# Larger TensorE blocks for the first two batches' scores, the token fold and the row transposes of a fused attention and FFT-mixing kernel

## The chip, the cores and the metric

One core of one Trainium2 chip runs one launch of the kernel. The metric is the device time of that launch in microseconds (us), median of several runs. The kernel is a program written out in full: every engine (TensorE = PE, VectorE = DVE, ScalarE = ACT, GpSimd = POOL, SyncE = SP) has one long in-order list of instructions, with semaphores between them.

## The reference

Four batches, eight heads, 768 tokens, head size 64. Attention with a window of 96 tokens and 8 global tokens and a linear distance penalty; then, on the attention's output x (4 x 768 x 512), a two-dimensional FFT whose real part is added to x, a normalisation over the 512 features, and a two-layer network of 2048 hidden units.

```python
scores = scale * q @ k.T - slope[h] * dist          # kept: 0 <= i-j < 96, or j < 8
a = softmax(where(keep, scores, -1e9)); x = a @ v    # heads side by side: [B, 768, 512]
u = x + real(fft(fft(x, axis=1), axis=2))
un = (u - mean(u)) / sqrt(var(u) + 1e-6)
out = u + relu(un @ w_ch1) @ w_ch2
```

## The kernel before

**Stages.** For each batch b the work is: transposes of q and k (`trans`), scores and exponentials (`score`), weighted sums (`av`), a token fold of x (`fold_0` for batch 0, `fold_s` for the others) and a feature fold (`fold_d`), two DFT stages (`y_unit`, `u_unit`), transposes of the normalised rows (`nt_unit`), and the two layers (`ph_unit`, `pg_unit` or `pg_units`). The batches overlap: while the layers of one batch fill TensorE, the attention of the next is put between them. Heads are handled in pairs: hp = 0..3, and pair number n = 4 b + hp.

**What sets the order.** A table `ORDER` in the class `Plan` names, for every engine, its units or operations in sequence. PE's names are units: A is attention, M is the fold and DFT work, H the first layer, G the second. `A37` is the 38th attention unit; `M0.1` is the second operation that unit M0 asks of ACT or DVE. The tables are fixed. `Plan.run` only walks through them with prices for each operation; the prices decide in which of several PSUM buffers a unit's result goes, not the order on an engine. An engine waits at the head of its list until what that instruction needs is there.

**PSUM.** Before the layers start, four double banks ("xx" 0 and 1, "C", "D") serve all units in turn. A unit of PE can start when the bank it is given has been emptied by ACT or DVE.

**Scores of batches 0 and 1** (`score`, lines 704 to 782, with `pem` true). Each unit (b, hp, g) covers two of the six key blocks of 128 tokens (g = 0, 1, 2). The distance penalty is added by TensorE: four matmuls (line 729) in 64x64 blocks of the array multiply a scaled identity (`sid`) with a table of distances (`dist_sb`, both in the tile `misc`). Then the scores are added (line 743). The contraction is over 64 features, one head s of the pair in each half of the rows; the 128 keys of a block are cut into halves t, one in each half of the columns, so that four matmuls use four quarters of the array. For i > 0 the keys of the second 128 query columns come from `kB`, a copy of the keys with the global tokens put in (tile `mk`).

**Token fold of batch 0** (`fold_0`, lines 950 to 1039). Pairs 0 and 2 are folded by DVE (f1 to f4, with f5 on ACT). Pairs 1 and 3 (`PEF`) are folded by TensorE: for each of the two, unit `fold_pe(hp)` makes six sums of the six token blocks of x as 32 matmuls of 128 columns with a scaled identity as weights (line 1013), into one bank. M0 does pair 1, M1 pair 3. The result is copied out in two operations each (lines 1018 and 1020): M0.0, M0.1 and M1.0 on ACT, M1.1 on DVE. `norm` (lines 832 and 834) is the DVE operation that writes x of one pair, half of the token blocks at a time: A21.0 and A22.0 write pair 1, A23.0 and A24.0 pair 3.

**Order around the fold.** On PE: `... A23 A24 A37 A36 M0 A34 A25 M1 A35 M4 A28 A38 A26 M5 M2 ...`. A23 and A24 are the weighted sums of pair 3 of batch 0; A37 and A36 are scores of batch 1; A34 and A25 are transposes of batch 1; A35, A28 and A38 are scores of batch 1; M4 and M5 (`spread_unit`) place x for later; M2 is the first DFT unit. On DVE: `... A17.0 A22.0 A21.0 T.75 T.73 T.76 A23.0 A24.0 T.78 A34.1 T.79 T.74 T.80 M1.1 T.81 T.82 ...`, where T.80 and T.81 are the two halves of `g0`, the first step of the feature fold.

**Row transposes** (`nt_unit`, lines 1296 to 1324). For the three row groups of batch 0, 32 transposes of 64x64 blocks (line 1309) turn the normalised rows; the later groups are turned by DMA.

Of the kernel before, what the change touches and what calls it, by code (L numbers as in the profile page):

```python
# [24 lines left out]
class Plan:  # L25
# [9 lines left out]
    MIX = 1.3  # L35
    LANDED = {"HW": 0.55, "SW": 1.3}
    LAT = {"ACT": 0.14, "DVE": 0.12, "POOL": 0.08}
# [84 lines left out]
    def op_go(self, eng, name, start):  # L122
# [6 lines left out]
        if eng == "POOL":  # L129
            self.ports.append((start, end, 1 if dma else 0 if outs and outs[0][0] in ("vB", "kB") else 2))  # L130
        if dma:
            at = max(max(end + 0.55, 5.5) if eng == "POOL" else end + lat + 2.7 * (lat == 1.0 and end > 3.5), self.now)
# [19 lines left out]

    SHARED = {"kB": 1, "vB": 1, "sid": 1, "f1": 0, "f2": 0, "f3": 0, "z": 0, "g0": 0, "w": 0, "s": 0, "w2a": 0, "w2t": 0, "ex": 0}
# [3 lines left out]
    def beside(self, start, cost, kind):  # L157
# [4 lines left out]
        if names:  # L162
            s = self.op_start("POOL", names[-1])
            if s is not None:
                p = self.made[names[-1]]
                ports = ports + [(max(s, start), max(s, start) + p[0]["POOL"][0], 1 if p[7] else 0 if p[3] and p[3][0][0] in ("vB", "kB") else 2)]
# [15 lines left out]
    def move(self, go=False):  # L182
# [4 lines left out]
        both = [h[2] for k, h in act if k != "AQ" or sw]  # L187
        each = sum(both) * (self.MIX if len(both) > 1 else 1.0) / 1000.0
        rate = {k: h[2] / 1000.0 if k == "AQ" and not sw else each for k, h in act}
        t = min([self.now + h[1] * rate[k] for k, h in act] + [h[0] for k, h in heads if h[0] > self.now + 1e-9] + [self.NEVER])  # L190
        if not go:
            return t
# [3 lines left out]
        for k, q in self.q.items():  # L196
            if q and q[0][1] <= 1e-4:
                _, _, _, outs, uses, cell = q.pop(0)
                cell[0] = t + (1.3 + 0.4 * (t > 12) if k == "SW" else 1.1 if t < 8 else self.LANDED["HW"] + 0.7)
# [21 lines left out]
    def unit_start(self, unit):  # L221
# [7 lines left out]
        if not there:  # L229
# [114 lines left out]
def act(n):  # L344
    return 0.1 + n / 1180.0
# [10 lines left out]
def pool(n):  # L356
    return 0.16 + n / 1080.0


@with_exitstack  # L360
def kernel(
# [24 lines left out]
    PEF = (1, 3)  # L386
    CS = 2
# [130 lines left out]
    def load_v(b, hp):  # L518
        h0 = 2 * hp
        if b >= FB:  # L520
# [3 lines left out]
            swq(whole, 1.08, [("avdone", b - 2), ("wl", 7)], [("v", b, hp, t) for t in range(2)], (1536, 0.93), False)  # L524
            return
        if b == 1:
            for t in range(2 - hp % 2 * 2):
# [3 lines left out]
                swq(four, 1.08, [], [("v", b, hp, t), ("v", b, hp + 1, t)], (1536, 0.93))  # L531
            return
        for t in range(2):
# [3 lines left out]
            swq(run, 0.85, ([("avdone", b - 2), ("wl", 7)] if b > 1 else []), [("v", b, hp, t)], (768, 0.93), b < 2)  # L537
# [4 lines left out]
    def load_qk(b, hp):  # L542
# [3 lines left out]
        for w, src in enumerate((q, k)):  # L546
            if b >= FB:
                for h in range(2):
# [4 lines left out]
                    swq(run, 0.85, free(tag, ti) + [("wl", 7)], [("qk", n, w, h)], (768, 0.93), False)  # L553
# [25 lines left out]
            if n == 4:  # L579
# [5 lines left out]
                swq(two, 1.08, free(tag, ti), [("qk", n, w), ("qk", n + 1, w)], (1536, 1.53))  # L585
# [7 lines left out]
            swq(run, 0.85, free(tag, ti), [("qk", n, w)], (768, 1.53))  # L593
# [110 lines left out]
    def score(b, hp, g):  # L704
# [3 lines left out]
        def run(start, ring):  # L708
# [22 lines left out]
            for i, c0, cw in tiles:  # L731
                for s in range(2):
# [7 lines left out]
                    for q0, q1 in [(0, P), (P, 2 * P)][:cw // P] if i else [(0, 2 * P)]:  # L740
                        for t in range(2):
                            kt = kB[lo:lo + 64, n, i - 1, t, :] if q0 else TT[n][lo:lo + 64, 1, i * P + 64 * t:i * P + 64 * t + 64]
                            nc.tensor.matmul(pa[64 * t:64 * t + 64, s, c0 + q0:c0 + q1], kt,  # L743
                                             TT[n][lo:lo + 64, 0, i * P + q0:i * P + q1], start=not pem, stop=True,
                                             skip_group_check=pem, tile_position=(lo, 64 * t))
            e = pl.pe((0.45, 0.45, 0.34)[g] if pem else 0.24, start, "64x64" if pem else "64x32")
# [61 lines left out]
    def av(b, hp):  # L808
# [28 lines left out]
        def part(start, ring, x, k):  # L837
# [15 lines left out]
            pl.later([("DVE", 0.17 + 0.03 * m + m * dve(384), lambda: norm(po, k))], free(*XT[b]), e,  # L853
# [10 lines left out]
    def bounce(b):  # L864
# [26 lines left out]
        pl.later([("POOL", 1.1, rg)], xw + [("xr", b), ("c", "back")], 0.0, [("xg", b)], dma=(128, 4.94), rank=0)  # L891

    def fold_s(b):
# [3 lines left out]
        for n, (c0, cw) in enumerate(parts):  # L897
# [43 lines left out]
            pl.later([("DVE", (4 if b else 2) * dve2(cw), f3)], [("f2", b, n)], 0.0, [("f3", b, n)])  # L941
# [8 lines left out]
    def fold_0():  # L950
# [53 lines left out]
        def fold_pe(hp):  # L1004
            cols = slice(hp * P, (hp + 1) * P)

            def run(start, ring):
                zy()
                pf = bank(ring, f"pf_{hp}")
                for n, terms in enumerate(ZS):  # L1010
                    o = pf[:, n // 4, (n % 4) * P:(n % 4 + 1) * P]
                    for x, (w, i) in enumerate(terms):
                        nc.tensor.matmul(o, w, X[0][:, i, cols], start=(x == 0), stop=(x == len(terms) - 1))
                e = pl.pe(mm_us(P, 32), start)
                pl.used(("free",) + XT[0], e)
                zc = T[("z", 0)][:, :, cols]
                pv = pf.rearrange("p b (n m) -> p (b n) m", m=P)
                pl.later([("ACT", act(512), lambda: A(zc[:, 0:4], pv[:, 0:4], AF.Copy)), ("DVE", dve(512), lambda: V.tensor_copy(zc[:, 0:4], pv[:, 0:4]))],
                         [], e, [("z", 0, hp)], rank=0)
# [769 lines left out]
```

## Time and profile before

| what | value |
|---|---|
| time, median of 3 runs (lowest to highest) | 247.56 us (247.53 to 248.01) |
| the profiled execution: its time | 245.87 us |
| the profiled execution: span from first to last instruction | 244.1 us |
| mean granted TensorE clock in it | 0.991 |
| TensorE busy (matmuls) | 232.0 us, 3251 matmuls, and as many weight loads |
| DVE, ACT, POOL busy | 193.4, 138.8, 114.8 us |

The profile tells of one execution. "Busy" of PE is the time in which at least one matmul was under way from its first read to its modelled end, so that short pauses between groups do not show in it; the starts of the groups in the timeline do show them. A wait is put down to what released it; "issue" is time in which an engine waited for nothing that the profile knows of.

### The profile page before, as it was taken

The page shows a single profiled execution, that of the slowest core. Times are in us where ns is not written, and L with a number is a line of the kernel's source. Part 1 is how long each engine was busy: PE and PEld are TensorE (multiplying, and loading weights), DVE is VectorE, ACT ScalarE, POOL GpSimd, SP SyncE. Part 2 cuts the span into 40 slices and gives each one's busy share as a digit, 9 for nine tenths or more (in the row PEclk, how much of TensorE's full clock was granted, in tenths as well). Part 3 has the DMA queues.
Part 4 walks back from the last instruction along what each step waited for, and adds up shares of the span by engine and source line. Part 5 has one row for each costly group of instructions (what it writes and reads, how often), then busy time and mean ns, then how long its engine had stood idle before and what let it go on. Part 6 is the DMA issues. An engine that isn't in the chain of part 4 may idle for free.

```text
span 244.1 us, 7606 instructions
## 1 busy us (share of the span) xinstructions
PE 232.0 (95%) x3251; PEld 191.2 (78%) x3251; DVE 193.4 (79%) x420; ACT 138.8 (57%) x226; POOL 114.8 (47%) x164
## 2 busy tenths in 40 slices
PE   7679899999999999999999999999999999999993
PEld 2557776878677667788989888898889898888883
DVE  2559997879972789999999889889998755846483
ACT  2368788864657468658357788364534651434200
POOL 8998898866590038999059056500300320011020
PEclk9997999999999999999999999999999999999999
DMA  6999999999999999999999979220570330040212
GB/s 170 181 169 145 157 235 172 197 190 196 110 145 152 234 179 205 117 135 110 242 184 285 135 84 156 46 33 13 174 258 4 77 99 0 1 130 1 89 72 99
DMA packets 95938, 32.85 MB, mean 135 GB/s; under 512 B 84160, under 2 KB 92480, under 8 KB 95904
## 3 DMA queue, kind: packets, MB, share of 16 engines
q0 software_dynamic: 66176, 17.06, 71.7%
q1 hardware_dynamic: 26560, 12.56, 25.1%
q10 hardware_dynamic: 3168, 2.75, 4.1%
q8 instruction: 25, 0.41, 0.7%
q14 instruction: 9, 0.07, 0.1%
HBM read 31.44 MB, written 8.65 MB: 164 GB/s over the span
## 4 chain that ended last, share of the span: by engine, by line
PE 67%; DMA 14%; DVE 5%; ACT 5%; POOL 3%; issue 3%; SPq 1%; POOLq 0%
PE ph L1339 29%; PE pgD L1484 14%; PE pgA L1484 10%; DMA qk<-in_q_dram 4%; DMA v<-in_v_dram 4%; PE py L1105 3%; DMA hT<-in_q_dram 3%; PE pg L1370 3%; PE pav L822 3%; ACT ex L766 2%; DMA back<-backm 2%; DMA xr<-xd,back 2%; PE sc L737 2%; PE pu L1192 1%; ACT mk L1657 1%
## 5 line engine op out<-in xcount | busy, mean ns | idle before, releaser
L1339 PE MATMUL ph<-unT,w 128*128 128x256 f16 x768 | 94.4, 273 | 0.8 <-issue 0.4
L1339 PEld LDWEIGHTS <-w 128*128 128x128 f16 x768 | 73.6, 98 | 12.5 <-issue 1.2
L1344 ACT ACTIVATE hT<-ph 128x512 f16<-128x512 f32 x73 | 42.9, 596 | 54.6 <-PE ph L1339 52.6
L1484 PEld LDWEIGHTS <-hT 128*128 128x128 f16 x320 | 31.0, 98 | 4.3 <-issue 0.4
L1285 POOL TENSOR_SCALAR sm<-sm 128x2 f32<-128x2 f32 x12 | 3.4, 284 | 58.2 <-ACT un L1278 57.8
L763 ACT ACTIVATE er<-sc 128x1024 f16<-128x1024 f32 (+1 forms) x24 | 22.3, 951 | 11.4 <-PE sc L737 8.2
L1345 DVE TENSOR_SCALAR hT<-ph 128x512 f16<-128x512 f32 x23 | 15.7, 687 | 12.7 <-PE ph L1339 12.7
L766 ACT ACTIVATE ex<-sc 128x1024 f16<-128x1024 f32 (+1 forms) x24 | 21.7, 955 | 7.1 <-PE sc L743 6.9
L1502 DVE SCALAR_TENSOR_TENSOR u<-pgA,sm,u 128x256 f32<-128x256 f32 (+1 forms) x30 | 16.9, 568 | 6.4 <-PE pgA L1484 6.0
L1502 DVE SCALAR_TENSOR_TENSOR u<-pgD,sm,u 128x512 f32<-128x512 f32 (+1 forms) x21 | 15.2, 722 | 3.5 <-PE pgD L1484 3.3
L1355 POOL DMA_INDIRECT out_dram<-u,back x4 | 4.5, 1120 | 27.5 <-DVE rev L1140 16.3
L887 POOL DMA_INDIRECT xr<-xd,back x3 | 4.8, 1602 | 25.4 <-PE pg L1370 16.1
L1370 PE MATMUL pg<-w,hT 128*128 128x512 f16 x64 | 16.0, 379 | 0.0
L1118 ACT ACTIVATE zy<-py 128x1024 f16<-128x1024 f32 (+1 forms) x13 | 11.1, 857 | 8.4 <-PE py L1105 6.1
L778 DVE TENSOR_TENSOR ex<-er,mk 128x1024 f16<-128x1024 f16 (+1 forms) x24 | 15.1, 646 | 0.7 <-ACT er L763 0.7
L1278 ACT ACTIVATE un<-un 128x512 f16<-128x512 f16 x24 | 15.0, 625 | 1.1 <-DMA unT<-un 1.1
L552 POOL DMA_DIRECT2D qk<-in_k_dram x16 | 13.7, 903 | 1.2 <-DMA w<-in_moe_w_ch_dram 0.8
L1269 ACT ACTIVATE un<-u,sm 128x512 f16<-128x512 f32 x19 | 13.1, 717 | 1.9 <-DVE sm L1251 0.7
L552 POOL DMA_DIRECT2D qk<-in_q_dram x16 | 13.6, 870 | 0.0
L822 PEld LDWEIGHTS <-ex 128*128 128x128 f16 x352 | 12.4, 97 | 1.1 <-ACT ex L766 0.4
L834 DVE TENSOR_TENSOR x<-pav,rc 128x384 f16<-128x384 f32 x24 | 12.6, 554 | 0.6
L822 PE MATMUL pav<-v,ex 128*128 128x65 f16 x224 | 12.9, 193 | 0.2
(170 smaller groups left out, 492.9 us busy)
## 6 DMA issues: line engine op xcount, KB each, us to landing
w<-in_moe_w_ch_dram POOLq DMA_DIRECT2D x8, 512.0 KB, 13.4
out_dram<-u SPq DMA_DIRECT2D x15, 256.0 KB, 3.0
v<-in_v_dram POOLq DMA_DIRECT2D x12, 192.0 KB, 5.8
qk<-in_k_dram POOLq DMA_DIRECT2D x16, 96.0 KB, 5.4
qk<-in_q_dram POOLq DMA_DIRECT2D x16, 96.0 KB, 4.5
xr<-xd SPq DMA_DIRECT2D x3, 512.0 KB, 4.6
xd<-x ACTq DMA_DIRECT2D x2, 768.0 KB, 4.5
v<-in_v_dram POOLq DMA_DIRECT2D x8, 96.0 KB, 7.0
```

The costliest lines, as they stand in the source:

```text
L552: nc.gpsimd.dma_start(qk16[n][:, w, :, h], src[b, h0 + h].rearrange("(i m) d -> m i d", m=P))
L763: A(mine(), cut(pa), AF.Exp, 0.0, 0.125)
L766: A(cut(expst[hp][:, :, g * 512:g * 512 + (384 if g == 2 else 512)]), cut(pa), AF.Exp, 0.0, 0.125)
L778: VT(o, mine(), m, op=ALU.mult)
L822: nc.tensor.matmul(o[:, s * 65:(s + 1) * 65], lhsT, w, start=(a == 0), stop=(a == len(ops) - 1), skip_group_check=True)
L1278: A(x, x, AF.Square, accum_out=MV[c][:, a, 2:3])
L1339: nc.tensor.matmul(ph[:, a * CH:(a + 1) * CH].rearrange("p (x m) -> p x m", x=2), W1[0][:, d, jb * P:(jb + 1) * P], UNT[c][:, :, d, :], st ...
L1344: pl.later([("ACT", act(512), lambda: A(dst, ph, AF.Relu)), ("DVE", dve(512), lambda: V.tensor_scalar_max(dst, ph, 0.0))], [], e, [("h", c ...
L1345: ("DVE", dve(512), lambda: V.tensor_scalar_max(dst, ph, 0.0))],
L1370: nc.tensor.matmul(pg, HT[c][:, jb, t * P:(t + 1) * P], W2[0][:, jb, :], start=(jb == 0), stop=(jb == NJ - 1))
L1484: nc.tensor.matmul(o, lhs(j), rhs(j), start=(first and j == 0), stop=(j == NK - 1), skip_group_check=True)
L1502: V.scalar_tensor_tensor(o, x, r(t), acc, op0=ALU.mult, op1=ALU.add)
```

## The change

Three kinds of TensorE work are written in larger blocks.

1. *Scores of batches 0 and 1.* The score matmuls use blocks of 64 rows by 128 columns: one matmul covers all 128 keys of a block, where two covered 64 each. The penalty's four matmuls stay as they are, in 64x64 blocks. A unit has 12 matmuls instead of 20 (g = 1), or 10 instead of 16 (g = 0 and 2).
2. *Token fold of batch 0.* The two fold units no longer stand for a pair each. M0 makes the first four of the six sums for pairs 1 and 3 at once (24 matmuls of 256 columns), M1 the other two (8 of 256). M0 now needs x of both pairs. M0.0, M0.1 and M1.0, all on ACT, copy 512 columns each; DVE's M1.1 is gone.
3. *Row transposes.* Eight transposes of 128x128 in place of 32 of 64x64, into one bank, for three row groups.

That is 160 + 32 + 72 = 264 matmuls and 264 weight loads fewer. The tables of the order are otherwise the same. The prices of the planner are changed in many places (DMA rates and landings, ACT's fixed part, GpSimd's operations); they change no order, only which PSUM bank some units of batch 1 get. Two operations are offered to a further engine (`slow`, and `distk` on ACT), but no table names them there.

```diff
@@ score @@
-                    for q0, q1 in [(0, P), (P, 2 * P)][:cw // P] if i else [(0, 2 * P)]:
-                        for t in range(2):
-                            kt = kB[lo:lo + 64, n, i - 1, t, :] if q0 else TT[n][lo:lo + 64, 1, i * P + 64 * t:i * P + 64 * t + 64]
-                            nc.tensor.matmul(pa[64 * t:64 * t + 64, s, c0 + q0:c0 + q1], kt,
-                                             TT[n][lo:lo + 64, 0, i * P + q0:i * P + q1], start=not pem, stop=True,
-                                             skip_group_check=pem, tile_position=(lo, 64 * t))
-            e = pl.pe((0.45, 0.45, 0.34)[g] if pem else 0.24, start, "64x64" if pem else "64x32")
+                    own = TT[n][lo:lo + 64, 1, i * P:i * P + P]
+                    for q0, q1, kt in [(0, cw, own)] if i == 0 or cw == P else [(0, P, own), (P, cw, kB[lo:lo + 64, n, i - 1].rearrange("p t m -> p (t m)"))]:
+                        nc.tensor.matmul(pa[:, s, c0 + q0:c0 + q1], kt, TT[n][lo:lo + 64, 0, i * P + q0:i * P + q1],
+                                         start=not pem, stop=True, skip_group_check=pem, tile_position=(lo, 0))
+            e = pl.pe((0.65, 0.63, 0.44)[g] if pem else (0.33 if g == 0 else 0.21), start, "64x64" if pem else "64x32")
@@ fold_0 @@
-        def fold_pe(hp):
-            cols = slice(hp * P, (hp + 1) * P)
+        def fold_pe(part):
+            some = ZS[:4] if part == 0 else ZS[4:]
...
-                for n, terms in enumerate(ZS):
-                    o = pf[:, n // 4, (n % 4) * P:(n % 4 + 1) * P]
+                for n, terms in enumerate(some):
+                    o = pf[:, n // 2, (n % 2) * 256:(n % 2) * 256 + 256]
                     for x, (w, i) in enumerate(terms):
-                        nc.tensor.matmul(o, w, X[0][:, i, cols], start=(x == 0), stop=(x == len(terms) - 1))
+                        nc.tensor.matmul(o.rearrange("p (x m) -> p x m", x=2), w, X[0][:, i].rearrange("p (x y m) -> p x y m", y=2, m=P)[:, :, 1],
+                                         start=(x == 0), stop=(x == len(terms) - 1))
...
-            MIX.append(([("x", 0, hp, z) for z in range(2)] + [("sid", 1), ("hid",)], BANKS(0), run))
+            MIX.append(([("x", 0, hp, z) for hp in PEF for z in range(2)] + [("sid", 1), ("hid",)], BANKS(0), run))
@@ nt_unit @@
-                    for i in range(2):
-                        for h in range(2):
-                            r, o, x = slice(64 * i, 64 * i + 64), d * P + 64 * h, 64 * (a * ND + d)
-                            nc.tensor.transpose(pt[64 * h:64 * h + 64, i, x:x + 64], un[r, a, o:o + 64], idn[r, r],
-                                                tile_position=(64 * i, 64 * h))
+                    nc.tensor.transpose(pt[:, 0, (a * ND + d) * P:(a * ND + d + 1) * P], un[:, a, d * P:(d + 1) * P], idn)
@@ Plan.ORDER, DVE @@
-            "A24.0 T.78 A34.1 T.79 T.74 T.80 M1.1 T.81 T.82 A26.1 T.83 M2.1 M3.0 M9.1 M9.0 M7.0 M7.2 M7.1 M7.3 M8.0 M10.0 M8.2 M6.0 M11.0 M8.1 M8.3 M13.0 "
+            "A24.0 T.78 A34.1 T.79 T.74 T.80 T.81 T.82 A26.1 T.83 M2.1 M3.0 M9.1 M9.0 M7.0 M7.2 M7.1 M7.3 M8.0 M10.0 M8.2 M6.0 M11.0 M8.1 M8.3 M13.0 "
```

PE in one score unit (pair 0, g = 1), from the last of its four penalty matmuls on. Before:

```order
L729 MATMUL sc_1_207<-misc 64x512
L743 LDWEIGHTS qkT_170
L743 MATMUL sc_1_207<-qkT_170 64x128
L743 LDWEIGHTS qkT_170
L743 MATMUL sc_1_207<-qkT_170 64x128
L743 LDWEIGHTS mk
L743 MATMUL sc_1_207<-qkT_170,mk 64x128
L743 LDWEIGHTS mk
L743 MATMUL sc_1_207<-qkT_170,mk 64x128
```

And in the changed kernel (the first number of a shape is now 128, the keys of one matmul):

```order
L740 MATMUL sc_1_205<-misc 64x512
L753 LDWEIGHTS qkT_170
L753 MATMUL sc_1_205<-qkT_170 128x128
L753 LDWEIGHTS mk
L753 MATMUL sc_1_205<-qkT_170,mk 128x128
L753 LDWEIGHTS qkT_170
L753 MATMUL sc_1_205<-qkT_170 128x128
L753 LDWEIGHTS mk
L753 MATMUL sc_1_205<-qkT_170,mk 128x128
```

What was 64x64 throughout the unit now goes from 64x64 to 64x128 within it, and back at the next unit's penalty.

PE at the start of the first fold unit, M0, with the semaphores that an instruction waits for. Before:

```order
L743 MATMUL sc_1_690<-qkT_623,mk 64x128
L1013 LDWEIGHTS ident [waits DVE_49]
L1013 MATMUL pf_716<-x_383,ident 128x128 [waits PE_49]
L1013 LDWEIGHTS ident
L1013 MATMUL pf_716<-x_383,ident 128x128
```

And in the changed kernel:

```order
L753 MATMUL sc_1_610<-qkT_543,mk 128x128
L1023 LDWEIGHTS ident [waits DVE_49]
L1023 MATMUL pf_641<-x_343,ident 128x256 [waits PE_49]
L1023 LDWEIGHTS ident
L1023 MATMUL pf_641<-x_343,ident 128x256 [waits DVE_49]
```

The unit stands at the same place, and there is a second wait for DVE: the second matmul reads token block 3, which A24.0 writes for pair 3.

ACT around the fold. Before:

```order
L978 ACTIVATE zy_479<-ww_481 128x128 x2
L1018 ACTIVATE zy_479<-pf_716 128x4x128
L978 ACTIVATE zy_479<-ww_481 128x128 x2
L1020 ACTIVATE zy_479<-pf_716 128x2x128
L679 ACTIVATE qkT_861<-pt_800 128x1536
L1018 ACTIVATE zy_479<-pf_828 128x4x128
```

And in the changed kernel:

```order
L987 ACTIVATE zy_406<-ww_408 128x128 x2
L1034 ACTIVATE zy_406<-pf_641 128x4x128
L987 ACTIVATE zy_406<-ww_408 128x128 x2
L1034 ACTIVATE zy_406<-pf_641 128x4x128
L690 ACTIVATE qkT_733<-pt_696 128x1536
L1030 ACTIVATE zy_406<-pf_724 128x4x128
```

The sequence is the same; the fourth row copies 512 columns instead of 256, and the last is now the only copy of the second unit.

More of the change, by code (lines that the diff above doesn't have):

```diff
@@ L35 @@
     MIX = 1.3
+    ALONE = 1.54
     LANDED = {"HW": 0.55, "SW": 1.3}
-    LAT = {"ACT": 0.14, "DVE": 0.12, "POOL": 0.08}
+    LAT = {"ACT": 0.18, "DVE": 0.12, "POOL": 0.08}
     def __init__(self):
@@ L129, in op_go @@
         if eng == "POOL":
[L130 removed]
+            self.ports.append((start, end, 1 if dma else 0 if outs and outs[0][0] in ("vB", "kB", "ts", "w1s", "s") else 2))
         if dma:
[L132 removed]
+            at = max(max(end + 0.95, 5.33) if eng == "POOL" else end + lat + 2.7 * (lat == 1.0 and end > 3.5), self.now)
             cell = [self.NEVER]
@@ L190, in move @@
         t = min([self.now + h[1] * rate[k] for k, h in act] + [h[0] for k, h in heads if h[0] > self.now + 1e-9] + [self.NEVER])
+        if sw and nxt > self.now + 1e-9:
+            t = min(t, nxt)
         if not go:
```

108 lines of the change are left out of this document (60 added, 48 removed).

## The prediction

> **What bounds the kernel now.** I read the page's first part, then the windows of four stages, then PE's waits and its timeline up to 60 us.
>
> ```profile
> span 244.1 us, 7606 instructions
> PE 232.0 (95%) x3251; PEld 191.2 (78%) x3251; DVE 193.4 (79%) x420; ACT 138.8 (57%) x226; POOL 114.8 (47%) x164
> ...
> 36.00:56.00 20.00, 18.91 (x407) 14.92 (x402) 16.27 (x41) 15.49 (x23) 16.60 (x27) 1.00 1.87 186
> 56.00:76.00 20.00, 20.00 (x198) 14.76 (x197) 16.66 (x35) 11.34 (x23) 11.96 (x15) 1.00 1.76 147
> 106.00:240.00 134.00, 134.00 (x1603) 119.02 (x1599) 109.93 (x230) 67.53 (x119) 38.24 (x51) 1.00 0.60 104
> ```
>
> In a window's row the first number after the window is its length, the second PE's busy time; the last three are the granted clock, the DMA share and GB/s. From 56 us on PE is busy all the time, but for about 1 us between 76 and 106. So what arrives late at 56 us ends late by as much, and what counts is when PE gets there. All that is changed lies before, except two of the three groups of row transposes.
>
> Before 56 us PE has holes, and its waits name three without a releaser that matter, beside one for a DMA at the start:
>
> ```profile
> PE pt L652 <- DMA hT<-in_q_dram: 1.6, 1, 1.6
> PE pt L652 <- issue: 1.5, 1, 1.5
> PE py L1105 <- issue: 0.6, 1, 0.6
> PE ph L1339 <- issue: 0.4, 1, 0.4
> ```
>
> Counted in the timeline, the three stand after 223, 733 and 989 matmuls. The distances are 510 and 256, multiples of 128 but for two. Each matmul has a weight load, so 128 matmuls are 256 instructions: PE waits there for a block of its own program. The Trainium skill, "Runtime: NRT & Kernel Launch", section "Instruction fetch mechanics", says that an engine's program is refilled in blocks of 256 instructions and that the cost is mostly hidden. The trace agrees on the block and not on the hiding: the first hole is 1.53 us. Were it hidden, no hole could be saved, and the sum below would lose its two gains from holes and come to +3.05.
>
> ```profile
> 15.32 0.47 PE L652 MATMUL pt<-ident,hT 128*64 128x128 f16 x10
> 17.32 0.58 PE L652 MATMUL pt<-ident,hT 128*64 128x128 f16 x14 [1.53 <-issue]
> ...
> 14.42:17.83 3.41, 1.81 (x49) 1.37 (x45) 1.72 (x5) 2.01 (x3) 3.33 (x6) 1.00 2.27 163
> 17.83:21.24 3.41, 3.41 (x76) 2.40 (x76) 3.25 (x6) 2.44 (x3) 2.21 (x4) 0.50 1.98 164
> ...
> 17.95 0.96 DVE L676 COPY qkT<-pt 128x1536 f16<-128x1536 f16 x1 [1.74 <-PE pt L652]
> ```
>
> The hole cuts the transposes of pair 1 of batch 0 (A6) in two. DVE waits for them until 17.95 and has no pause after that until 30.2. And 3.41 us after the hole run at half clock.
>
> **The score blocks.** Four matmuls in 64x64 blocks, with 128 columns each, start every 0.055 us: the four quarters work at once.
>
> ```profile
> 43.10 0.36 PE L729 MATMUL sc<-misc 64*64 64x384 f16 x4
> ...
> 43.45 0.33 PE L729 MATMUL sc<-misc 64*64 64x384 f16 x4
> 43.61 0.23 PE L743 MATMUL sc<-qkT 64*64 64x128 f16 x4
> 43.67 0.23 PE L743 MATMUL sc<-qkT,mk 64*64 64x128 f16 x4
> 43.73 0.23 PE L743 MATMUL sc<-qkT 64*64 64x128 f16 x4
> 43.88 1.07 PE L1192 MATMUL pu<-t,zy 128*128 128x128 f16 x16
> ```
>
> In 64x128 blocks two work at once on twice the keys, which is the same rate if the two row halves overlap as they do now. So 160 pairs of instructions fewer save no array time. They add changes of block shape. Two units of the same kind stand here: the first, followed by another 64x64 unit, takes 43.45 - 43.10 = 0.35; the second, followed by 128x128 work, takes 0.43. A change of shape costs 0.08. It does so too where only the columns change:
>
> ```profile
> 29.47 0.86 PE L652 MATMUL pt<-ident,qk 128*64 128x128 f16 x24
> 30.16 0.84 PE L652 MATMUL pt<-ident,tt 128*64 128x128 f16 x24
> 30.93 0.56 PE L1013 MATMUL pf<-x,ident 128*128 128x128 f16 x7
> ```
>
> 24 transposes take 0.69 before more of the same shape, and 0.77 before 128x128. The Trainium skill, "TensorEngine Tiling (Array Packing)", section "Key Properties", says that a change of the tiling mode, not of the tile, drains TensorE; it gives no time. By it the change from the penalty's blocks to the scores' must cost something, and the trace's 0.08 agrees. I take 0.09, since two heads that run one after the other within a unit also leave a short tail at each drain. No row shows 64x64 to 64x128; bounds are 0 (a column switch at no cost) and 0.12 (the longest such step I find).
>
> Each of the 24 units gets one change more inside, and a second where the next unit also is in 64x64 blocks. After the fold there are ten units (A35 A28 A38 A39 A29 A32 A33 A40 A31 A27) and five such neighbours (A35-M4, A28-A38, A39-A29, A33-A40, A31-M6): 15 x 0.09 = **+1.35**.
>
> **The fold.** What matters is when it may start.
>
> ```profile
> 26.79 0.56 DVE L834 TENSOR_TENSOR x<-pav,rc 128x384 f16<-128x384 f32 x1
> 28.70 0.56 DVE L834 TENSOR_TENSOR x<-pav,rc 128x384 f16<-128x384 f32 x1
> 29.40 0.56 DVE L834 TENSOR_TENSOR x<-pav,rc 128x384 f16<-128x384 f32 x1
> 30.44 0.96 DVE L676 COPY qkT<-pt 128x1536 f16<-128x1536 f16 x1 [0.22 <-PE pt L652]
> ...
> 27.58:29.47 1.89, 1.89 (x32) 1.78 (x32) 1.00 1.40 195
> 55.20 1.75 PE ph L1339 x16
> ```
>
> The last rows are the first fold unit's stretch and the chain's piece of 16 layer matmuls of 256 columns. The columns to work through are the same: 64 matmuls of 128 in two units of 1.89, or 32 of 256. At 1.75/16 = 0.109 us, 24 take 2.62 and 8 take 0.87, with a change of shape each 3.67 for 3.78: **-0.1**.
>
> M0 starts at 27.58, right after pair 1 is written (26.79 + 0.56 = 27.35). Now it needs pair 3 too, whose last write ends at 29.96: 2.38 later. Behind the waiting M0 stand, on PE's list, A34, A25, M1 and all that follows; DVE needs A34's result for the copy at 30.44 and then idles, ACT needs A25's. Nothing can pass, so this goes straight to the end unless DVE gets there earlier.
>
> It does, by the first hole. In the changed kernel A6 ends after 197 matmuls, so that it lies wholly ahead of the 223rd, where the hole now is; by then two more score units are issued, and the block has had more time to come. A6 then needs 24 x 0.028 = 0.67 from its start. Its start moves back: six score units ahead of it have ten changes of shape, 0.9, of which I let 0.5 count, since some of these units wait for ACT or DVE anyway. It ends near 16.5 in place of 17.7, and DVE, without a pause from there on, can be 1.1 earlier at A24.0 if the last v of batch 0 is there when DVE comes to copy it.
>
> ```profile
> 16.23 0.75 POOL L535 DMA_DIRECT2D v<-in_v_dram  x1
> ...
> DMA to landing us min/median/max: 5.8/7.0/7.4
> ...
> 23.70 0.29 DVE L793 COPY vB<-v 128x528 f16<-128x528 f16 x1
> ```
>
> It is issued at 16.23, so it lands from 22.0 to 23.6; DVE would come at 22.6. I let the 1.1 stand: M0 starts near 28.9, **+1.3**. Bounds: +2.4 (no gain from the hole) and +0.7 (all of 1.7 us).
>
> The order of the rest fits: with M0 done at 31.6 and M1 at 34.1, ACT's copies run about 2 us later than now, DVE's g0 too, and the first DFT unit finds its banks and its operands at about 38.7, when PE comes to it (37.23 now).
>
> **What is given back.** Between the starts of A28 and A38 lie 1.18 us:
>
> ```profile
> 33.93 0.39 PE L729 MATMUL sc<-misc 64*64 64x512 f16 x4
> ...
> 35.11 0.41 PE L729 MATMUL sc<-misc 64*64 64x512 f16 x4 [0.32 <-DVE zy L1020]
> ```
>
> A28's matmuls need 0.44 (four of 512 columns at once, 0.215, and four times 0.055). A38 waits for the bank that M1.1 empties; M1.1 is gone, and M1.0 empties it on ACT at about 35.6, before PE comes there (36.4). Of the 0.74 I take back **-0.4**; the rest is a wait for a copy of keys, which may stay. Bounds 0 and -0.7.
>
> The holes of 0.56 and 0.38 us: fewer instructions per microsecond leave more time for each block, but the boundary at the 733rd matmul falls among layer matmuls only 6 us after the one before, and the hole at the 989th came 6.6 us after its predecessor. One of two stays: **-0.5**. Bounds 0 and -0.94.
>
> The row transposes:
>
> ```profile
> 47.02 0.47 PE L1309 MATMUL ptu<-ident,un 64*64 64x64 f16 x32
> 47.42 0.28 PE L1192 MATMUL pu<-t,zy 128*128 128x128 f16 x2
> 53.83 0.45 PE L1309 MATMUL ptu<-ident,un 64*64 64x64 f16 x32
> 54.36 0.33 PE L822 MATMUL pav<-v,ex 128*128 128x65 f16 x5
> ```
>
> A group takes 0.40 to 0.53 now. Eight of 128 columns at 0.056 (a fold unit's 1.89 less a change, over 32) take 0.45, and two groups lose the change of shape on entering: **-0.2** in all.
>
> Sum: +1.35 - 0.1 + 1.3 - 0.4 - 0.5 - 0.2 = +1.45. The profiled execution's own time is 245.87 (span 244.1 and 1.77 around it); it becomes 247.3. The median of the runs is 247.56, 1.69 above that execution; with it the forecast is **249.0 us**.
>
> **The rivals.**
>
> *The row halves don't overlap in 64x128 blocks.* For it: nothing in the trace runs in such blocks. Against it: row halves overlap in the 64x64 units. The scores of a unit would take twice their 0.22 (g = 0, 1) or 0.165 (g = 2): after the fold 7 x 0.22 + 3 x 0.165 = 2.0, and the units before A6 would undo the 1.1 gained there. 249.0 + 3.1 = 252.1. Chance 0.12.
>
> *The wait ahead of the fold slows the clock.* PE, done with A36 near 26.7, idles until 28.9. The window with the 1.53 us hole was followed by 3.41 us at 0.50; a second such stretch costs up to 1.7: 250.7. Against it: the 1.6 us for the DMA ended at 9.48 and were not followed by one:
>
> ```profile
> 8.00:16.00 8.00, 6.09 (x184) 4.69 (x184) 5.29 (x12) 5.52 (x7) 7.88 (x15) 1.00 2.05 170
> ```
>
> The Trainium skill, "TensorE: Matmul & The Clock Gate", Part 1, asks a whole idle window of about 3.4 us for this, by which there would be none; the row at 17.83 speaks against that rule, since its predecessor was half busy. Chance 0.18.
>
> *Faster: the switch from the penalty to the scores is free.* Only the column split changes there, and the rows keep theirs. If it costs under 0.03, the 1.35 goes and A6 ends another 0.5 earlier; with the second of the later holes gone too (0.44): 249.0 - 2.3 = 246.7. Against it: 29.47 to 30.93 above. It decides once the price is below 0.03. Chance 0.20.
>
> *Nothing to measure:* the waits around 28 to 36 us absorb the fold's wait, as DVE's chain turns out 1 us earlier still. 247.6. Chance 0.08.
>
> **How the numbers follow.** Forecast 249.0 with chance 0.42, its own range 248.1 to 250.0. Half a microsecond (0.2%) is about what this measurement can tell from none. Faster 0.20 (the free switch), same 0.09 (the last rival and a little of the forecast), slower 0.71 (forecast, clock, row halves). The range reaches down to the free switch, 246.5, and up past the slower clock, 251.4, leaving out the row halves and the outer parts.
>
> **What would show it.** The timeline should have the first fold matmuls after a PE wait of 1 us or more for DVE's L843, starting near 29; DVE's copy of A6 near 16.7; a hole of issue after the 223rd matmul under 0.5 us and no half clock before 21; 0.08 to 0.1 us between the last penalty matmul's columns and the first score; 0.055 us between starts of pairs of 64x128 matmuls. It is wrong if M0 starts before 28.3, if that step is under 0.03, or if A6 is cut by a hole again.

## The result, and the profile after

| kernel | median of the runs, us | runs | to before, with its 95% interval |
|---|---|---|---|
| before | 247.55 (244.93 to 250.14) | 14 | |
| changed | 250.16 (249.02 to 252.95) | 14 | 1.0144 (1.0104 to 1.0183) |

By the medians the change makes the kernel 2.6 us slower; by the ratio it is 1.44%, or 3.6 us. Here and below, medians count all runs, while the ratio leaves out runs more than 1.5% above the fastest of their kernel, so that a tail of late runs shows in the median alone. The first two rows of the changed kernel's page:

```profile
span 250.6 us, 7075 instructions
PE 237.1 (95%) x2987; PEld 190.6 (76%) x2987; DVE 193.6 (77%) x419; ACT 138.6 (55%) x226; POOL 114.2 (46%) x164
```

There are 531 instructions fewer, and PE is busy 5 us longer. The profiled execution is one of the longest of its 14 (252.34 us), so its 6.5 us over the profiled execution of before are not the median's 2.6. Part of the rest is found below.

PE's waits, with the engine and the line waited for, then us in all, times and the longest:

```profile
PE pf L1023 <- DVE x L843: 2.4, 2, 2.0
...
PE pav L831 <- ACT unT L1329: 1.1, 1, 1.1
PE sc L748 <- DVE u L1262: 0.8, 1, 0.8
```

Two things stand out. No row with "issue" is left among PE's waits, where before had 2.5 us in the three main ones. And the fold now waits for the division of pair 3; further on, two units wait that did not before. The timeline of PE, start and length in us, then what it does and in brackets the idle time ahead of it:

```profile
26.69 0.41 PE L740 MATMUL sc<-misc 64*64 64x512 f16 x4
27.04 0.23 PE L753 MATMUL sc<-qkT 64*128 64x128 f16 x2
27.10 0.22 PE L753 MATMUL sc<-qkT,mk 64*128 64x128 f16 x2
27.16 0.22 PE L753 MATMUL sc<-qkT 64*128 64x128 f16 x2
27.21 0.22 PE L753 MATMUL sc<-qkT,mk 64*128 64x128 f16 x2
29.43 0.28 PE L1023 MATMUL pf<-x,ident 128*128 128x256 f16 x1 [1.99 <-DVE x L843]
30.12 0.81 PE L1023 MATMUL pf<-x,ident 128*128 128x256 f16 x6 [0.41 <-DVE x L843]
...
32.84 0.42 PE L1023 MATMUL pf<-x,ident 128*128 128x256 f16 x1
33.05 0.42 PE L1023 MATMUL pf<-x,misc 128*128 128x256 f16 x1
33.26 0.42 PE L1023 MATMUL pf<-x,hid 128*128 128x256 f16 x1
```

The same stretch by windows (length, PE's busy time with its matmuls, and so on; the granted clock is the third number from the end):

```profile
27.44:29.43 1.99, 0.00 (x1) 0.01 (x1) 1.96 (x10) 1.54 (x4) 1.99 (x4) 1.00 1.49 177
29.43:31.05 1.62, 1.22 (x10) 0.94 (x11) 0.86 (x4) 0.00 (x0) 1.62 (x3) 1.00 0.95 132
31.05:34.46 3.41, 3.41 (x20) 2.16 (x20) 0.00 (x0) 0.10 (x1) 0.55 (x1) 0.50 1.11 267
34.46:36.77 2.31, 2.31 (x56) 1.94 (x52) 1.46 (x3) 2.18 (x5) 0.44 (x1) 1.00 2.51 198
```

PE stands still from 27.44 to 29.43. 1.6 us after it has begun again it runs at half clock for 3.41 us, just while the fold is in work: its matmuls start 0.21 us apart (32.84, 33.05, 33.26), where 0.109 was expected. With the wait of 0.41 for pair 3's second division, the first fold unit takes 4.8 us until the transposes behind it start (34.25). VectorE and ScalarE meanwhile run dry, as the row of VectorE's copy behind it shows; the others are what decides when the fold may start:

```profile
17.41 0.95 DVE L687 COPY qkT<-pt 128x1536 f16<-128x1536 f16 x1
20.06 0.30 DVE L802 COPY vB<-v 128x528 f16<-128x528 f16 x1 [0.76 <-DMA v<-in_v_dram]
...
28.81 0.56 DVE L843 TENSOR_TENSOR x<-pav,rc 128x384 f16<-128x384 f32 x1
...
29.51 0.56 DVE L843 TENSOR_TENSOR x<-pav,rc 128x384 f16<-128x384 f32 x1
...
35.31 0.96 DVE L687 COPY qkT<-pt 128x1536 f16<-128x1536 f16 x1 [4.98 <-PE pt L663]
```

The last division of pair 3 ends at 29.51 + 0.56 = 30.07. It ended at 29.96 before: in this execution VectorE has gained nothing.

PE's loss against before, taken at the starts of the same unit in the two profiled executions, is 1.2 us at 13.8 us: half of it, 0.61, is there at the transposes that wait for a DMA at the start (10.09 for 9.48), the rest comes from five changed score units. It is -0.5 at 23.7, since the first hole and before's half clock behind it are gone, +1.85 at the first fold unit, +4.8 at the transposes behind it (0.9 of this is only work that moved from the second fold unit into the first), +4.0 at the first DFT unit, +3.6 at the second row transposes, +4.8 at the pav that follows, +5.1 at 140.9 us, +6.1 at 141.4 and 6.5 at the end (times of the kernel before).

### The profile page after: what moved, and what is told of

It is laid out like the page before. It is cut to its first block, busy times and chain, and to the rows that moved or that the text cites. A ratio compares the mean times of both kernels' runs of the same rounds, so it can differ in the third digit from the quotient of the medians.

```text
span 250.6 us, 7075 instructions
## 1 busy us (share of the span) xinstructions
PE 237.1 (95%) x2987; PEld 190.6 (76%) x2987; DVE 193.6 (77%) x419; ACT 138.6 (55%) x226; POOL 114.2 (46%) x164
## 4 chain that ended last, share of the span: by engine, by line
PE 68%; DVE 14%; DMA 12%; POOL 2%; ACT 2%; issue 1%; DVEq 0%; SPq 0%
PE ph L1349 26%; PE pgD L1497 12%; PE pgA L1497 9%; PE pav L831 3%; DMA xd<-tt 3%; DMA v<-in_v_dram 3%; PE pg L1380 3%; PE py L1119 3%; DMA out_dram<-u 3%; PE pz L1659 2%; PE pu L1206 2%; DMA unT<-un 2%; DMA xr<-xd 2%; PE pf L1023 2%; DVE u L1515 2%; PE sc L748 1%
## 5 line engine op out<-in xcount | busy, mean ns | idle before, releaser
L1299 POOL TENSOR_SCALAR sm<-sm 128x2 f32<-128x2 f32 x12 | 4.8, 400 | 64.8 <-ACT un L1292 64.5
L787 DVE TENSOR_TENSOR ex<-er,mk 128x1024 f16<-128x1024 f16 (+1 forms) x24 | 15.7, 669 | 1.1 <-ACT er L772 1.1
L896 POOL DMA_INDIRECT xr<-xd,back x3 | 3.6, 1196 | 25.0 <-PE ph L1349 16.5
L687 DVE COPY qkT<-pt 128x1536 f16<-128x1536 f16 (+1 forms) x6 | 5.3, 887 | 10.0 <-PE pt L663 6.8
```

The costliest lines, as they stand in the source:

```text
L787: VT(o, mine(), m, op=ALU.mult)
```

## The experiments

Two theories stood at first: F, that the fold, as one unit for both pairs, carries the loss, and S, that the changes of shape in the score units do. Each kernel ran beside runs of before on the same chip. "Clock loss" is one minus a run's mean granted clock, times its time, averaged over the runs: a stretch of 3.41 us at 0.50 counts 1.7 us. It is 1.05 us for before (96 runs beside the experiments; two more, at 302 and 598 us, are left out) and 2.19 us for the changed kernel (14 runs).

| experiment | median, us | before beside it | ratio and interval | clock loss, us | runs |
|---|---|---|---|---|---|
| fold alone | 251.81 | 247.66 | 1.0160 (1.0115 to 1.0204) | 2.65 | 6 |
| scores alone | 247.55 | 247.66 | 0.9993 (0.9960 to 1.0026) | 1.22 | 12 |
| row transposes alone | 247.28 | 247.66 | 1.0011 (0.9977 to 1.0046) | 0.78 | 12 |
| changed, fold by pairs | 249.20 | 247.66 | 1.0046 (1.0002 to 1.0091) | 1.13 | 12 |
| changed, fold two units later | 250.87 | 248.15 | 1.0107 (1.0032 to 1.0182) | 1.67 | 6 |
| changed, wait filled | 248.99 | 248.15 | 1.0070 (1.0035 to 1.0104) | 0.44 | 12 |
| changed, norms swapped | 249.78 | 248.15 | 1.0116 (1.0056 to 1.0176) | 2.05 | 6 |
| prices alone | 247.81 | 248.15 | 1.0004 (0.9960 to 1.0048) | 0.62 | 12 |
| changed, pair 3 divided first | 250.04 | 248.05 | 1.0059 (1.0016 to 1.0102) | 1.23 | 12 |
| the same, and norms swapped | 248.89 | 248.05 | 1.0000 (0.9959 to 1.0042) | 0.52 | 13 |
| before, pair 3 divided first | 247.15 | 248.05 | 0.9957 (0.9925 to 0.9989) | 0.95 | 12 |
| scores and row transposes | 248.86 | 246.94 | 1.0034 (0.9987 to 1.0081) | 0.92 | 12 |

### Which of the three parts costs the time

Four kernels take the change apart. Three make one part of it in the kernel before, at before's prices:

```diff
fold alone:            + fold_pe(hp // 2), two units of 256 columns, and no M1.1 on VectorE
scores alone:          + nc.tensor.matmul(pa[:, s, c0 + q0:c0 + q1], kt, ..., tile_position=(lo, 0))
row transposes alone:  + nc.tensor.transpose(pt[:, 0, ...], un[:, a, d * P:(d + 1) * P], idn)
```

The fourth is the changed kernel with before's fold:

```diff
- fold_pe(hp // 2)
+ fold_pe(hp)
```

> The kernel before with the new token fold alone (24 + 8 matmuls of 256 columns, M0 after both pairs). Theory F (the loss is the wait ahead of the fold and the half clock that follows it): M0 waits 2 us or more for the last write of x of pair 3, a stretch of 3.4 us at half clock may follow, and the time is 2 to 4 us over that of before. Theory S (the loss is the changes of block shape in the score units): no more than 0.5 us over.

> The kernel before with the scores of batches 0 and 1 in 64x128 blocks alone. Theory S: a step of 0.13 us within each of 24 units and 0.10 between neighbours, about 4.5 us in all, of which 2 to 3 us reach the end. Theory F: the ten units after the fold add 1.8 us, the program's holes that go give 1 us or more back, and the time is within 1 us of before.

> The kernel before with the row transposes in 128x128 blocks alone. Both theories: 0 to 0.5 us faster, three groups of 0.45 us without a change of block shape on either side.

> The changed kernel with the fold put back to one unit for each pair (scores, transposes and prices as changed). Theory F: 2 to 4 us under the changed kernel, about the time of before. Theory S: within 1 us of the changed kernel, 249 to 251 us.

The fold alone loses 4.15 us by the medians, a little more than theory F had said and more than the whole change; by the ratios (1.0160 and 1.0144) the two can't be told apart. Scores alone, where theory S wanted 2 to 3 us, and row transposes alone move nothing that can be measured. The fourth kernel is less clear: its ratio falls from 1.0144 to 1.0046, which is 2.4 us and what theory F said, but its median is only 1.0 us below the changed kernel's, in the range of theory S. So the fold by itself carries the loss, as theory F has it, and the score blocks by themselves do not; what is left with before's fold is taken up under "Scores and row transposes together". The fold-alone kernel's waits show what it has besides the fold's wait:

```profile
PE pf L1014 <- DVE x L834: 2.1, 2, 1.7
...
PE pav L822 <- issue: 1.5, 1, 1.5
...
PE pt L652 <- issue: 0.9, 1, 0.9
PE ptu L1314 <- issue: 0.9, 1, 0.9
```

It has the wait ahead of the fold and keeps holes of issue as well, and its clock loss is the largest of all, 2.65 us. The trace of scores alone has no hole: with the pairs of instructions that the blocks save, the holes go. The other traces agree. In the five kernels with before's score blocks (before itself, fold alone, row transposes alone, prices alone, before with pair 3 divided first) every hole of 0.2 us or more stands after 223, 350, 733, 861 or 989 matmuls, whatever unit is there; the distances are multiples of 128 but for one or two. In the nine with the new blocks there is none. That scores alone is no faster all the same fits the changes of shape: 24 units at 0.13 us for the change inside (26.69 to 27.04 in the timeline above, less 0.215 for the matmuls) are 3.1 us, part of it beside other waits, against holes of 2.5.

### Is it the wait, and can the wait be filled with other work?

The two fold units go behind the two units of transposes that stood behind the first of them, and ScalarE's copies with them:

```diff
 PE:  A37 A36
- M0 A34 A25 M1
+ A34 A25 M0 M1
 ACT:
- T.72 M0.0 T.77 M0.1 A25.1 M1.0
+ T.72 T.77 A25.1 M0.0 M0.1 M1.0
```

> The changed kernel with both fold units placed two units later on TensorE: behind the 48 transposes of A34 and A25 (1.4 us of work that needs no fold), with ScalarE's copies of the fold moved behind its copy for A25. Theory W (the loss is TensorE standing still until pair 3 is divided, 2.0 + 0.4 us, with the half clock that follows it): the wait falls to 0.5-1.0 us, the copies of A34 and A25 on VectorE and ScalarE start about 4 us earlier, and the median is 247.0-248.5, within 0.5% of before. Rival G (the fold in one piece costs the loss wherever it stands, by banks and later waits): 250, as the changed kernel.

It came out at 250.87: the expectation of theory W missed, and rival G's 250 came near. VectorE's copy of A34 does start 4.9 us earlier (30.37 for 35.31), but nothing is gained by it. The timeline of its PE shows where the wait went:

```profile
28.76 0.86 PE L663 MATMUL pt<-ident,qk 128*64 128x128 f16 x24 [1.20 <-ACT ex L775]
30.24 0.53 PE L663 MATMUL pt<-ident,tt 128*64 128x128 f16 x12 [0.62 <-DVE x L843]
31.04 0.74 PE L663 MATMUL pt<-ident,tt 128*64 128x128 f16 x12 [0.27 <-DMA tt<-in_k_dram]
31.70 1.68 PE L1023 MATMUL pf<-x,ident 128*128 128x256 f16 x7
```

The transposes wait for their bank, 1.20 us for ScalarE's exponential and 0.62 for the division that empties the other bank, and then 0.27 for a DMA: 2.1 us in all, where the fold had waited 2.4. And 3.41 us at half clock follow here too, from 31.20 on. So, by this trace, the wait belongs to the stretch, not to the fold's place in it. That the kernel before could go on there because its first fold unit needed pair 1 alone, and the bank that pair 1 had left, is how the order reads; it was not tried.

### Is part of it the clock?

```diff
 pf = bank(ring, f"pf_{part}")
+for _ in range(0 if part else 10):
+    nc.tensor.matmul(pf[:, 0, :], EG[:, 0, 0:P], EG[:, 0], start=True, stop=True)
```

> The changed kernel with ten matmuls of 512 columns of zeros ahead of the first fold matmul, into its bank, which the fold then overwrites: TensorE works through its 2 us wait (10 x 0.213 = 2.13 us), nothing else is moved. Theory C (part of the loss is the half clock that follows the idle time): the first real fold matmul still comes near 29.5, but the twelve-matmul unit then takes about 2.7 us in place of 4.8, there is no half clock between 30 and 35, and the median is 248.7-249.3. Rival I (only the idle time counts, the half clock comes anyway or costs nothing): 250.2, as the changed kernel.

```profile
26.45 2.33 PE L1020 MATMUL pf<-eg 128*128 128x512 f16 x10
28.62 0.27 PE L1025 MATMUL pf<-x,ident 128*128 128x256 f16 x1
29.05 0.81 PE L1025 MATMUL pf<-x,ident 128*128 128x256 f16 x6 [0.16 <-DVE x L843]
...
31.65 0.86 PE L663 MATMUL pt<-ident,qk 128*64 128x128 f16 x24
```

With ten matmuls on zeros in the wait, from 26.45 on, the first fold unit takes 31.65 - 28.62 = 3.0 us, and there is no half clock behind it; over 12 runs the clock loss is 0.44 us instead of 2.19. That the fold starts 0.8 us earlier than in the changed kernel's profiled execution is not the filling's doing: VectorE's list is ahead already at A6's copy (16.79 for 17.41). The median is 1.2 us lower than the changed kernel's, where theory C expected it, and the ratio 0.7% lower, which fits the 1.75 us by which the clock loss fell; the two intervals just touch. Theory C holds, and its rival falls: the idle time of 2 us costs 1.2 us or more by the clock behind it, on the average of runs that have it and runs that don't.

### The bank behind the second row transposes

Before the change, the second row transposes and the pav behind them had different banks. The fold, now in two units that empty their banks otherwise, leads the planner to give both the same one (fold alone has the wait below too, 1.1 us; no kernel with before's fold has it):

```profile
57.44 0.61 PE L1320 MATMUL ptu<-ident,un 128*128 128x128 f16 x8
59.16 0.37 PE L831 MATMUL pav<-v,ex 128*128 128x65 f16 x7 [1.11 <-ACT unT L1329]
```

The pav waits until ScalarE has copied the transposes out. Dividing pair 3 of batch 1 ahead of pair 2 frees another bank:

```diff
- T.85 A43.0 H4.0 H3.0 A44.0
+ T.85 A44.0 A43.0 H4.0 H3.0
```

> The changed kernel with one entry of VectorE's list moved: pav of pair 3 of batch 1 is divided ahead of pair 2, so that its bank is free earlier and the transposes of rows get another bank than the pav that follows them. Theory B (0.8-1.1 us of the loss is that pav waiting for ScalarE's copy out of its own bank, near 58 us): the wait on unT is gone from TensorE's waits and the median is 249.0-249.5. Rival: the copy's time is waited for elsewhere a little later, 250.2.

```profile
56.56 0.61 PE L1320 MATMUL ptu<-ident,un 128*128 128x128 f16 x8
57.28 0.39 PE L831 MATMUL pav<-v,ex 128*128 128x65 f16 x7
```

The wait is gone from the trace (the pav now follows after 0.72 us, it was 1.72), and the median is 249.78, 0.4 us lower, with a ratio whose interval overlaps the changed kernel's; it lies between the 249.0 to 249.5 of theory B and the rival's 250.2. The trace shows 1.0 us gained at that place; how much of it reaches the end, these six runs don't say.

### The planner's prices

The diff changes many of the planner's prices as well. This kernel has them, and none of the three parts:

```diff
+ ALONE = 1.54
- LAT = {"ACT": 0.14, "DVE": 0.12, "POOL": 0.08}
+ LAT = {"ACT": 0.18, "DVE": 0.12, "POOL": 0.08}
...
```

> The kernel before with the planner's new prices alone; all three code changes are undone. The order of every engine is that of before, and a few score units get another bank. Theory: 247.6, no change (within 0.3%). Rival P (the new banks cost what the per-pair variant still lost): 248.5-249.

247.81 against 248.15: the prices cost nothing that can be measured.

### Dividing pair 3 earlier

VectorE does six fold operations of pairs 0 and 2 ahead of pair 3's divisions. They are put behind:

```diff
- T.75 T.73 T.76 A23.0 A24.0
+ A23.0 A24.0 T.75 T.73 T.76
```

> The changed kernel with pair 3 of batch 0 divided 1.2 us earlier on VectorE: its two divisions stand ahead of the six fold operations of pairs 0 and 2 (27.38 to 28.59) instead of behind them. Theory W (the fold waits for nothing but this division): the first fold matmul starts 1.2 us earlier, near 28.2, the wait falls from 2.4 to about 1.2 us, the half clock behind it comes less often (average clock loss under 1.5 us instead of 2.2), and the median is 248.3-249.3. Rival: pair 3's pav on TensorE or the six operations moved back are waited for instead, 250.2.

> As the variant with the early division, and the norm of pair 3 of batch 1 ahead of pair 2's as well, so that the rows' transposes get another bank than the pav behind them. Both theories: the wait on unT is gone too, 0.4 to 0.8 us under the variant with the early division alone, 247.8-248.8; not faster than before, since the score blocks' changes of shape stay. Rival: below before, under 247.0, if the fetch holes that the change removes are worth more than those.

> The kernel before with the same move on VectorE's list (pair 3 divided ahead of the six fold operations). Before's first fold unit needs pair 1 alone, so theory W says that the move gains nothing here: 247.3-247.9, the same. Rival (the early division is worth its 1.2 us in any kernel): 246.5.

PE's timeline of the first of the three kernels:

```profile
27.78 0.28 PE L1023 MATMUL pf<-x,ident 128*128 128x256 f16 x1 [0.78 <-DVE x L843]
28.47 1.44 PE L1023 MATMUL pf<-x,ident 128*128 128x256 f16 x6 [0.41 <-DVE x L843]
```

The wait fell to 0.78 + 0.41 us, as expected, and the clock loss from 2.19 to 1.23 us. The ratio fell from 1.0144 to 1.0059, but the median, 250.04, is outside what was expected: half of the twelve runs are above 250 us. In the profiled execution even this shorter wait has half clock behind it (28.26 to 31.67; the six matmuls of the second row take 1.44 us, 0.81 in the changed kernel's). With the norms swapped as well, the ratio is 1.0000 and the median 248.89, 1.15 lower than without the swap and 0.1 above the range expected, with five of 13 runs above 250. In this kernel's profiled execution, the longest of its runs (254.34 us), a wait of VectorE late in the program stands out. Its timeline, VectorE and SyncE:

```profile
138.18 0.34 SPq L1616 DMA_DIRECT2D out_dram<-u  x1
...
145.63 0.85 DVE L1258 SCALAR_TENSOR_TENSOR u<-pu,xr 128x384 f32<-128x384 f32 x1 [3.48 <-DMA out_dram<-u]
```

The same two in the kernel before:

```profile
132.60 0.34 SPq L1603 DMA_DIRECT2D out_dram<-u  x1
...
137.46 0.87 DVE L1244 SCALAR_TENSOR_TENSOR u<-pu,xr 128x384 f32<-128x384 f32 x1 [0.44 <-DMA out_dram<-u]
```

VectorE needs a buffer whose rows are still on their way out: 3.48 us idle, and a score unit of PE behind it for 1.7. From the last store that SyncE issued ahead of it to its release it was 7.5 us here and 4.9 us in before. The changed kernel's profiled execution has the same wait, 2.58 us of VectorE and the 0.8 of PE for L1262. This is a part of its 6.5 us (the step of 1.0 between 140.9 and 141.4 us) that its other runs need not have. What makes the store late was not tried.

In the kernel before the same move is worth 0.43%, though theory W expected nothing: 247.15 us, between its 247.3 to 247.9 and the rival's 246.5. It is the only version that beats before with an interval clear of 1 (0.9925 to 0.9989), by little, and one of twelve such intervals can be so by chance. In before's trace a score unit waited 0.74 us beyond its matmuls from 33.93 on. Here the same unit is followed after 0.65 us instead of 1.18:

```profile
35.87 0.39 PE L729 MATMUL sc<-misc 64*64 64x512 f16 x4
...
36.52 0.41 PE L729 MATMUL sc<-misc 64*64 64x512 f16 x4
```

That could be the gain, if there is one; it was not tried by itself.

### Scores and row transposes together

The changed kernel with before's fold had come out 0.46% above before, though neither part alone, nor the prices, cost anything that could be measured. So the two parts were made together in the kernel before, the fold and the prices as they were:

```diff
+ nc.tensor.matmul(pa[:, s, c0 + q0:c0 + q1], kt, ..., tile_position=(lo, 0))
+ nc.tensor.transpose(pt[:, 0, ...], un[:, a, d * P:(d + 1) * P], idn)
```

> The kernel before with the score blocks and the row transposes changed together; the fold stays in units of one pair and the planner's prices stay as they were. Each of the two alone moved nothing, and so did the prices alone. Theory F (the whole loss lies in the fold): 247.4-248.1, the same as before within 0.3%, and the 249.2 of the per-pair variant was chance or its tail of late runs. Rival (the two together cost what each alone does not, about 1.1 us): 249.0-249.4.

The median is 248.86, between the 247.4 to 248.1 of theory F and the rival's 249.0 to 249.4, and the ratio's interval holds 1 (0.9987 to 1.0081). But five of the twelve runs lie above 250 us, as do five of the twelve of the variant with the fold by pairs, against five of 96 of before. The lower seven (245.57 to 249.16) lie where before lies. So the two together seem to spread the time upwards. Four of these ten late runs have a mean clock of 1.00, so the clock can't be all of it. The late store could be in it, but this kernel's profiled execution has one too (VectorE waits 2.20 us, PE 0.7) and is, with 246.00 us, one of its shortest. The cause stays open.

## Why the prediction held, and where its steps did not

The time of 250.16 us lies in the range (246.5 to 251.4) and on the side that was given 0.71, 1.2 us above the forecast. The sum had +1.45; the medians show +2.6.

**The fold's wait: place right, size at the upper end.** It was to start near 29 after a PE wait of 1 us or more for L843, and it does, at 29.43 after 1.99 us. The step that failed in this execution is the 1.1 us that VectorE was to gain, "if the last v of batch 0 is there": pair 3's last write ends at 30.07, where about 28.9 was forecast, so the term is the +2.4 of its upper bound and not +1.3. The score units ahead of A6 cost it 0.54 us, near the 0.5 taken. But the program's start was 0.61 late, so that the copy of A6 starts at 17.41 (17.95 before, 16.7 forecast), and then VectorE waits 0.76 us for a v at 20.06, an earlier one than the prediction looked at. Other executions differ in both. The variant with the norms swapped is the same program up to this place; in its profiled execution VectorE waits for no v (two rows of VectorE, then one of PE):

```profile
17.12 0.95 DVE L687 COPY qkT<-pt 128x1536 f16<-128x1536 f16 x1
...
28.76 0.56 DVE L843 TENSOR_TENSOR x<-pav,rc 128x384 f16<-128x384 f32 x1
...
28.68 0.28 PE L1023 MATMUL pf<-x,ident 128*128 128x256 f16 x1 [1.99 <-DVE x L843]
```

There the last write ends at 29.32, and in the variant with the filled wait at 29.00: 0.64 and 0.96 earlier than before, most of the 1.1. So the term was between about +1.4 and +2.5 from one execution to the next. PE's wait is 1.99 us all the same: PE waits for VectorE ahead of the fold as well (0.27 us for L804 at 25.31 and 0.20 for L843 at 26.13 in the changed kernel), so an earlier VectorE only brings PE to the fold the earlier.

**The clock: the rival came with the forecast.** The half clock behind the wait had been given 0.18 and up to 1.7 us as a case of its own, at 250.7, which is nearer to the 250.16 than the forecast is; it was argued against by the wait for a DMA at the start that had none behind it. It was the usual case: in 12 of 14 runs of the changed kernel the mean clock is 0.993 or less, which is one whole stretch, against 42 of 96 of before. Filling the wait took 1.2 us off, so this is shown. The rule of the Trainium skill ("TensorE: Matmul & The Clock Gate", Part 1), that the clock falls after a whole idle window of about 3.4 us, would have forbidden it; the trace does not agree, since 1.99 us of idle time were followed by 3.41 us at 0.50.

**A term that was missing.** That the fold's new use of the banks would put the second row transposes and the pav behind them into one bank was not seen: +1.2 us in the trace (from the second row transposes to the pav, against before), 0.4 in the medians of the experiment and 1.15 between the two kernels that divide pair 3 first.

**The holes: right in kind, too small.** The sum took one of the two later holes back, -0.5, and let the first leave up to 0.5. In the trace all three are gone: the gain between 39 and 54 us alone is 0.80 at the DFT unit and 0.65 at the layer piece ahead of the second row transposes. No hole stands behind the 223rd matmul, A6 is in one piece, and there is no half clock before 21, as the prediction had asked for; it used that for VectorE's start only; on PE it shows as the step from +1.2 to -0.5 us between 13.8 and 23.7 us, and the fold's wait then takes it back.

**The changes of shape: nearly right.** From the starts of the ten score units after the fold to the next unit's, less their matmuls, there are 2.7 us after and 1.4 before, in the two profiled executions. That is +1.3 with the unit between 33.93 and 35.11, which gave back 0.25 (0.4 was taken), so +1.55 without it, where the sum had +1.35. The change inside a unit is larger than the 0.09 taken: from 26.69, four matmuls of 512 columns at once take 0.215 and end at 26.91, and the first score starts at 27.04, 0.13 later. The other change, to the next unit, is 0.10. The rival of a free switch falls.

**The row halves overlap**, as forecast: the starts at 27.04, 27.10, 27.16 and 27.21, two matmuls each, are 0.055 apart. The rival at 252.1 falls.

**The fold's matmuls and the row transposes.** At full clock, as in the filled variant, the first unit takes 3.0 us with its shape change and a 0.16 us wait, the second 0.98 in the changed kernel: 3.8 without the wait, where the prediction had 3.67. A group of row transposes takes 0.45 (51.26 to 51.71), as forecast, but the -0.2 for all of them is not there: with the unit ahead of it the first group takes 1.10 us after and 1.01 before, the third 2.20 and 2.22.

So the sum came near because its errors cancel in part: a wait, a clock and a bank worth more than was put down, and holes worth more as well. That is luck in part, and a range of 4.9 us helped. The mechanism that decided the direction, the fold waiting for pair 3, was forecast.

## What to carry to other kernels

Joining two units into one makes the joined unit wait for the later of the two inputs; before counting what it saves, find which unit kept the engine going while the other input was on its way, and whether any other work has a free bank to take its place. An idle time of TensorE of 2 us can cost more than half as much again by the clock behind it, and meaningless matmuls in the wait take that part back. A part that measures as nothing may be a gain and a loss of one size (here, by the traces, holes against changes of shape), so it can look different beside another change.

## What the hardware showed that was not expected

An idle time of TensorE well under the length of one half-clock stretch (1.99 against 3.41 us) was enough to bring one on, and it began only 1.6 us after work had been taken up again. The clock records of the traces show a beat in it: the half clock begins at 31.05, which is 7 x 3.413 us after the rise to full clock at 7.16; before the change it begins at 17.83, 4 x 3.413 after 4.17; and in fold alone two such stretches begin at 23.91 and 30.74, 2 x 3.41 apart. This would explain why not every run has it: what may count is how much of the wait falls into one beat (27.64 to 31.05 held 1.22 us of PE's work). How little work is too little stays open. In the kernel with pair 3 divided first and the norms swapped, half clock followed a beat with 2.20 us of work (25.71 to 29.12) and did not follow one with 1.72 (145.17 to 148.58).

A store of rows that takes 4.9 us from issue to release in one execution took 7.5 in another, and 6.6 in the changed kernel's (138.44 to 145.00).
